# Folding the first MLP weight into Nyström attention, with coarser loads and merged attention pieces

## The chip, the core and the metric

The kernel runs on one core of one Trainium2 chip. The metric is device time in microseconds (us) for one execution. Each number for a kernel is the median of several executions; its profile is one further execution under the hardware profiler.

Engine names in the profile: PE is TensorE (matmuls), PEld its weight loads, DVE VectorE, ACT ScalarE, POOL GpSimd, SP the sync engine that issues some transfers. "L98" is line 98 of the kernel that the line comes from. The profile also records the clock granted to TensorE, 1.0 being full speed. In the code, PSUM tiles are what the matmuls write, and a tile's first dimension, 128 at most here, is its partitions.

## The reference

The operation is Nyström attention (8 batches, 8 heads, 576 tokens, 64 features per head, 32 landmarks) followed by an MLP with a squared ReLU (512 to 2048 to 512 features). Cut to what matters:

```python
q_lm = q.reshape(B, H, 32, 18, D).mean(axis=3)      # landmarks: means of 18 tokens
k_lm = k.reshape(B, H, 32, 18, D).mean(axis=3)
A  = softmax(q    @ k_lm.T / 8)      # 576 x 32
Bm = softmax(q_lm @ k_lm.T / 8)      # 32 x 32
C  = softmax(q_lm @ k.T    / 8)      # 32 x 576
Z  = Bm.T / (norm_1(Bm) * norm_inf(Bm) + 1e-6)      # 1-norm, inf-norm
for _ in range(6):                   # Newton steps towards the inverse of Bm
    Z = 2 * Z - Z @ Bm @ Z
x  = (A @ Z @ C @ v)                 # per head; then heads side by side: 4608 x 512
h  = x @ w_in                        # 4608 x 2048
return (relu(h) ** 2) @ w_out        # 4608 x 512
```

## The kernel before

Each batch of attention forms `xT` (x transposed, in bf16) for 576 tokens; the MLP then runs over nine blocks of 512 tokens. A "quad" is four heads whose 32 landmarks fill the 128 partitions. Inside a quad the Newton steps work on one 128x128 block-diagonal matrix.

The MLP block: MLP-in is 64 matmuls (4 feature tiles x 16), MLP-out is another 64. Both take their PSUM tile from the same two buffers ("mo").

```python
    def moe_superblock(t0, ntok):
        gT = moep.tile([P, D_FF // P, TOK_SB], BF16, tag="gT", bufs=1)
        for f in range(D_FF // P):
            hps = psum.tile([P, TOK_SB], F32, tag="mo", bufs=2)
            for kt in range(D_MODEL // P):
                nc.tensor.matmul(hps[:, 0:ntok], lhsT=w_in_bf[:, kt, f*P:(f+1)*P],
                                 rhs=xT[:, kt, t0:t0+ntok], start=..., stop=...)
            ... relu on ScalarE into r_sb, square on VectorE into gT[:, f, :] ...
        for ts0 in range(0, ntok, P):
            ops = psum.tile([P, D_MODEL], F32, tag="mo", bufs=2)
            ... 16 matmuls gT x w_out_bf, ScalarE copy, store ...
```

The loads: q and k come as bf16 through the software queue in pieces of 64 elements; v comes as f32 through the sync engine and is cast on VectorE.

```python
        for c in range(NCH):                       # 4 chunks of 128 tokens, one of 64
            nc.gpsimd.dma_start(qbf[:rows, c, :, :], q[b, :, s0:s0+rows, :].rearrange("h s d -> s h d"))
            ... the same for kbf ...
        vstg = qkv.tile([P, NCH, H, D], F32, tag="vstg")
        nc.vector.memzero(vstg[64:128, NCH - 1, :, :])
        for c in range(NCH):
            nc.sync.dma_start(vstg[:rows, c, :, :], v[b, ...])
        nc.vector.tensor_copy(v_aug[:, :, :, 0:D], vstg[:])
```

The attention works head by head on 32 partitions where it fills or reads the diagonal blocks:

```python
            BDB = quadp.tile([P, P], F32, tag="BDB")
            nc.vector.memzero(BDB[:])
            for h4 in range(4):
                nc.vector.tensor_scalar(out=BDB[32*h4:32*h4+32, 32*h4:32*h4+32],
                    in0=Ebm[32*h4:32*h4+32, :], scalar1=rrb[32*h4:32*h4+32, :], op0=ALU.mult, ...)
            # ... Newton steps; then, for C v:
            for g in range(4):
                nc.vector.reciprocal(rrc[32*g:32*g+32, :], cvps[32*g:32*g+32, ...])
            for g in range(4):
                nc.vector.tensor_scalar(out=cvq[32*g:32*g+32, :], in0=cvps[32*g:32*g+32, ...],
                                        scalar1=rrc[32*g:32*g+32, :], op0=ALU.mult, ...)
            nc.vector.memzero(wbd[:])
            for i in range(2):
                wps = ...                              # one matmul
                nc.scalar.copy(wbd[64*i:64*i+32, 0:D], wps[0:32, :])
                nc.scalar.copy(wbd[64*i+32:64*i+64, D:2*D], wps[32:64, :])
```

The softmax here doesn't subtract the row's maximum and nothing guards it: scores larger than these inputs give would overflow.

## Time and profile before

| | before |
|---|---|
| median of 4 runs | 468.79 us (466.21 to 471.53) |
| median in the rounds beside the changed kernel (16 runs) | 470.28 us |
| span of the profiled execution | 467.4 us |
| mean granted clock of TensorE | 0.963 |

These are lines of the profile page of the kernel before. The first gives the span, the second busy time, share of the span and instruction count of each engine; then comes TensorE's busy share in 40 slices of 11.7 us in tenths, and the sizes of the transfers' packets.

```profile
span 467.4 us, 7392 instructions
PE 395.1 (85%) x2720; PEld 196.3 (42%) x2720; DVE 259.1 (55%) x803; ACT 199.7 (43%) x541; POOL 71.5 (15%) x92
...
PE   0215678999989998999899989997989898999996
...
DMA packets 120324, 32.98 MB, mean 71 GB/s; under 512 B 113120, under 2 KB 115168, under 8 KB 120288
```

TensorE looks busy for 85% of the time, but "busy" counts each matmul's full duration in the trace: a matmul of 32 columns is recorded as 0.19 us long, where dense ones start 25 ns apart. A better measure is what dense matmuls need. The end of the run has nothing but the MLP. This is the timeline of TensorE there (start, duration, engine, line, operation, output and inputs, shape, count):

```profile
407.90 13.99 PE L98 MATMUL hps<-xT,w_in_bf 128*128 128x512 bf16 x64
421.72 13.98 PE L112 MATMUL ops<-w_out_bf,gT 128*128 128x512 bf16 x64
```

From start to start, 64 matmuls of 512 columns take 13.82 us: 216 ns each. The Trainium skill, page "TensorE: Matmul & The Clock Gate", section "Wait — 56ns, not 53.3ns?", gives N / 2.4 GHz + 2.5 ns per matmul of N columns with a floor near 25 ns. The trace agrees: 216, 56 and 25 ns for 512, 128 and 32 columns. I call the sum of these costs over all matmuls the **issue work**. It is an estimate (the few f32 matmuls are counted like bf16, and matmuls that start together are counted one by one): 324.6 us before. The rest of the span, 142.8 us, is **lost**: TensorE waits, or runs at a lower clock.

Where it is lost, by stretches: 50.6 us in the first 57 us, 32.7 us from 57 to 155 us, 11.6 us in the steady period of 48.5 us after that, 10.7 to 11.1 us in each of the next four. The two stretches of that first steady period follow, from the windows view of the kernel before. The columns are the stretch, its length, busy time and count of PE, PEld, DVE, ACT and POOL, the granted clock, the DMA share and GB/s.

```profile
155.04:169.00 13.96, 13.96 (x66) 6.23 (x65) 2.32 (x6) 2.35 (x5) 0.00 (x0) 1.00 0.60 142
169.00:203.50 34.50, 30.74 (x261) 16.10 (x261) 28.91 (x93) 20.63 (x61) 8.39 (x10) 0.95 0.56 43
```

The first stretch is MLP-out, one dense block, with 0.3 us lost. The second holds attention with MLP-in between: 23.3 us of issue work in 34.5 us, 11.2 us lost. VectorE is busy for 28.91 of those 34.5 us.

What happens in the start is shown by TensorE's longest wait there (view of waits: who waited for whom, us in total, times, longest) and by the timeline of VectorE before it:

```profile
PE bmps L183 <- DVE BD L173: 11.0, 1, 11.0
```
```profile
12.67 1.62 DVE L152 CAST v_aug<-vstg 128x2560 bf16<-128x2560 f32 x1 [5.78 <-DMA vstg<-in_v_dram]
...
33.59 1.49 DVE L152 CAST v_aug<-vstg 128x2560 bf16<-128x2560 f32 x1 [9.24 <-issue]
...
35.74 0.42 DVE L172 CAST BD<-means_ps 64x256 bf16<-64x256 f32 x1
```

The means were done by 25.07 us, but their copy (BD) started only after the second cast of v had run. That cast is for batch 1 (the cast for batch 0 ran at 12.67 us); the last of the transfers that it needs landed at 33.51 us. So attention of batch 0 cannot begin its scores before 35.7 us: it waits in VectorE's queue for a load that it does not need. Most of the 25 us before that went on waiting for q and k; the last piece of k landed at 24 us.

### The profile page before, as it was taken

Reading aid. Unit: us, or ns where it says so; the run is one execution under the profiler, and the core shown is the slowest. Engines: PE = TensorE matmul, PEld = TensorE weight load, DVE = VectorE, ACT = ScalarE, POOL = GpSimd, SP = SyncE. Lnnn points to the kernel's source line nnn. Section 1 sums busy time; section 2 is a strip of 40 time slices with the busy share of each in tenths; the row PEclk is TensorE's granted clock in tenths of the full one; section 3 lists DMA queues with packets and bytes.
Section 4 is the critical chain, followed back from the end, with each engine's and each line's share of the span. In section 5 each row is a group of like instructions: output and inputs, shape, how many; then the busy total and the mean of one; then the engine's idle time right before and its main releaser. Section 6 shows DMA issues by size and latency. Waiting matters only on the chain.

```text
span 467.4 us, 7392 instructions
## 1 busy us (share of the span) xinstructions
PE 395.1 (85%) x2720; PEld 196.3 (42%) x2720; DVE 259.1 (55%) x803; ACT 199.7 (43%) x541; POOL 71.5 (15%) x92
## 2 busy tenths in 40 slices
PE   0215678999989998999899989997989898999996
PEld 0013345344534543444354435443535443444442
DVE  4128578782678448853886288719750976041220
ACT  1012335562556254634463357325742574272541
POOL 8412070070007000600052003300000000000000
PEclk9999988799989998999899989999999989999999
DMA  9999999096109810991069204920002000101101
GB/s 157 169 194 158 185 176 132 2 95 153 46 1 86 142 67 1 61 165 69 1 45 72 78 1 29 75 82 9 1 1 87 5 1 1 67 24 45 45 25 67
DMA packets 120324, 32.98 MB, mean 71 GB/s; under 512 B 113120, under 2 KB 115168, under 8 KB 120288
## 3 DMA queue, kind: packets, MB, share of 16 engines
q0 software_dynamic: 77600, 13.64, 37.7%
q1 hardware_dynamic: 42688, 18.88, 17.7%
q8 instruction: 21, 0.34, 0.3%
q14 instruction: 15, 0.12, 0.1%
HBM read 36.70 MB, written 9.44 MB: 99 GB/s over the span
## 4 chain that ended last, share of the span: by engine, by line
PE 62%; DVE 17%; ACT 9%; DMA 4%; issue 4%; SPq 2%; DVEq 0%; ACTq 0%
PE ops L112 27%; PE hps L98 19%; DMA vstg<-in_v_dram 4%; PE tps L278 3%; PE ntp L250 2%; SPq L148 2%; PE ntp L246 2%; DVE stn L256 2%; PE o L362 2%; DVE rse L306 2%; DVE cvq L339 2%; DVE anorm L311 2%; ACT kT L286 2%; ACT Usb L249 2%; ACT r_sb L106 2%
## 5 line engine op out<-in xcount | busy, mean ns | idle before, releaser
L98 PE MATMUL hps<-xT,w_in_bf 128*128 128x512 bf16 x576 | 165.4, 398 | 1.6 <-ACT r_sb L106 1.4
L112 PE MATMUL ops<-w_out_bf,gT 128*128 128x512 bf16 x576 | 125.9, 379 | 0.1
L106 ACT ACTIVATE r_sb<-hps 128x512 bf16<-128x512 f32 x144 | 85.5, 603 | 39.6 <-PE hps L98 25.9
L107 DVE TENSOR_TENSOR gT<-r_sb 128x512 bf16<-128x512 bf16 x144 | 59.2, 422 | 46.6 <-ACT r_sb L106 45.2
L112 PEld LDWEIGHTS <-gT 128*128 128x128 bf16 x576 | 56.3, 98 | 67.8 <-DVE gT L107 0.5
L98 PEld LDWEIGHTS <-w_in_bf 128*128 128x128 bf16 x576 | 53.9, 102 | 45.8 <-issue 10.7
L135 POOL DMA_DIRECT2D qbf<-in_q_dram x40 | 35.9, 897 | 207.1 <-PE tps L278 201.7
L120 ACT COPY o_sb<-ops 128x512 f32<-128x512 f32 x36 | 21.1, 586 | 102.8 <-PE ops L112 102.8
L284 DVE COPY qT<-tps 128x640 bf16<-128x640 bf16 x32 | 15.4, 488 | 62.2 <-PE tps L278 61.1
L249 ACT CAST Usb<-ntp 128x128 bf16<-128x128 f32 x96 | 25.2, 266 | 47.3 <-PE ntp L246 45.5
L139 POOL DMA_DIRECT2D kbf<-in_k_dram x40 | 35.2, 880 | 14.5 <-DMA w_in_bf<-in_moe_w_in_dram 9.4
L256 DVE SCALAR_TENSOR_TENSOR stn<-stn,ntp 128x256 bf16<-128x256 bf16 x64 | 26.2, 421 | 11.8 <-PE ntp L253 6.3
L246 PE MATMUL ntp<-stn,BDBT_sb 128*128 128x128 bf16 x80 | 19.9, 248 | 7.6 <-DVE stn L256 6.5
L250 PE MATMUL ntp<-stn,Usb 128*128 128x128 bf16 x80 | 19.9, 257 | 7.5 <-ACT Usb L249 6.5
L250 PEld LDWEIGHTS <-Usb 128*128 128x128 bf16 x96 | 9.9, 103 | 37.2 <-ACT Usb L249 36.1
L286 ACT COPY kT<-tps 128x640 bf16<-128x640 bf16 x32 | 22.2, 697 | 7.4 <-PE tps L278 7.2
L369 DVE CAST xT<-o 128x512 bf16<-128x512 f32 x32 | 21.8, 691 | 5.4 <-PE o L362 4.3
L278 PE MATMUL tps<-ident_bf,kbf 128*128 128x128 bf16 x160 | 17.1, 234 | 6.1 <-DMA kbf<-in_k_dram 6.1
L161 PE MATMUL means_ps<-seg_bf,qbf 128*128 128x32 bf16 x160 | 9.2, 180 | 14.1 <-DMA qbf<-in_q_dram 13.9
L152 DVE CAST v_aug<-vstg 128x2560 bf16<-128x2560 f32 x8 | 12.0, 1503 | 15.1 <-issue 9.2
L339 DVE TENSOR_SCALAR cvq<-cvps,rrc 32x64 bf16<-32x64 f32 x64 | 18.0, 281 | 1.9
L172 DVE CAST BD<-means_ps 64x256 bf16<-64x256 f32 x8 | 3.3, 412 | 26.2 <-ACT STk L169 26.2
(85 smaller groups left out, 429.8 us busy)
## 6 DMA issues: line engine op xcount, KB each, us to landing
out_dram<-o_sb SPq DMA_DIRECT2D x36, 256.0 KB, 2.0
vstg<-in_v_dram SPq DMA_DIRECT2D x32, 256.0 KB, 6.3
qbf<-in_q_dram POOLq DMA_DIRECT2D x32, 128.0 KB, 4.5
kbf<-in_k_dram POOLq DMA_DIRECT2D x32, 128.0 KB, 4.6
w_in_bf<-in_moe_w_in_dram POOLq DMA_DIRECT2D x1, 2048.0 KB, 22.3
w_out_bf<-in_moe_w_out_dram POOLq DMA_DIRECT2D x1, 2048.0 KB, 24.5
vstg<-in_v_dram SPq DMA_DIRECT2D x8, 128.0 KB, 6.4
qbf<-in_q_dram POOLq DMA_DIRECT2D x8, 64.0 KB, 4.1
```

The source lines that it names most:

```text
L98: nc.tensor.matmul(hps[:, 0:ntok], lhsT=w_in_bf[:, kt, f * P:(f + 1) * P], rhs=xT[:, kt, t0:t0 + ntok], start=(kt == 0), stop=(kt == D_MOD ...
L106: nc.scalar.activation(r_sb[:, 0:ntok], hps[:, 0:ntok], AF.Relu)
L107: nc.vector.tensor_tensor(gT[:, f, 0:ntok], r_sb[:, 0:ntok], r_sb[:, 0:ntok], ALU.mult)
L112: nc.tensor.matmul(ops[0:m, :], lhsT=gT[:, f, ts0:ts0 + m], rhs=w_out_bf[:, f, :], start=(f == 0), stop=(f == D_FF // P - 1),)
L135: nc.gpsimd.dma_start(qbf[:rows, c, :, :], q[b, :, s0:s0 + rows, :].rearrange("h s d -> s h d"),)
L139: nc.gpsimd.dma_start(kbf[:rows, c, :, :], k[b, :, s0:s0 + rows, :].rearrange("h s d -> s h d"),)
L246: nc.tensor.matmul(Ups[:, :], lhsT=BDBT_sb[:, :], rhs=BDZ, start=True, stop=True)
L249: nc.scalar.copy(Usb[:], Ups[:])
L250: nc.tensor.matmul(VTps[:, :], lhsT=Usb[:, :], rhs=BDZT, start=True, stop=True)
L256: nc.vector.scalar_tensor_tensor(out=stn[:, :], in0=st[:, :], scalar=2.0, in1=ntp[:, P:3 * P], op0=ALU.mult, op1=ALU.subtract)
L278: nc.tensor.transpose(tps[:, 128 * c:128 * c + 128], tbf[:, c, 2 * p:2 * p + 2, :].rearrange("p h d -> p (h d)"), ident_bf[:],)
L286: nc.scalar.copy(tT[:], tps[:])
```

## The change

The intent: x is never needed by itself. With A the normalized scores and W = Z C v, h = A (W w_in), so w_in can be folded into attention: G = (Z C v) w_in per batch has 256 landmark rows (8 heads x 32), and the first GEMM contracts over 256 rows instead of 512 features. The same rewrite changes more:

- q, k and v are loaded with four consecutive tokens per partition ("(p c)"), in runs of 1 KB in memory, all as bf16 through the software queue; VectorE reorders q and k with one copy each; the output is stored in the same token order.
- Both quads share ops where possible. The per-head pieces on 32 partitions become one op on 128 partitions with a mask.
- MLP-out has a PSUM buffer of its own; one MLP-in tile holds 576 tokens; two batches share nine output tiles.

The diff, cut to its core (names shortened where the kernel unpacks them):

```diff
-            nc.gpsimd.dma_start(qbf[:rows, c, :, :], q[b, :, s0:s0+rows, :].rearrange("h s d -> s h d"))
-            nc.sync.dma_start(vstg[:rows, c, :, :], v[b, ...])          # f32, cast later
-        nc.vector.tensor_copy(v_aug[:, :, :, 0:D], vstg[:])
+            nc.gpsimd.dma_start(raw[:], src[b, :, 0:512, :].rearrange("h (p c) d -> p h c d", c=4))
+            nc.vector.tensor_copy(nat[:, 0:4, :, :], raw.rearrange("p h c d -> p c h d"))
+        nc.gpsimd.dma_start(vm[:], v[b, :, 0:512, :].rearrange("h (p c) d -> p h c d", c=4))
...
-            for h4 in range(4):
-                nc.vector.tensor_scalar(out=BDB[32*h4:32*h4+32, 32*h4:32*h4+32], ...)
+            nc.vector.scalar_tensor_tensor(out=st[:, 1, :, :], in0=spread(Bn, qd),
+                    scalar=rc[:, qd:qd+1], in1=blk[:], op0=ALU.mult, op1=ALU.mult)
...
-            for g in range(4): nc.vector.reciprocal(rrc[32*g:32*g+32, :], ...)
-            for g in range(4): nc.vector.tensor_scalar(out=cvq[32*g:32*g+32, :], ...)
+            nc.vector.reciprocal(rc2[:], cv[:, 4*D:4*D+1])
+            nc.vector.scalar_tensor_tensor(out=cvb[:], in0=cv[:, 0:4*D]..., scalar=rc2[:],
+                    in1=mask4..., op0=ALU.mult, op1=ALU.mult)
...
-            o512 = A-transposed x W per head pair, copied to xT
+        for n in range(4):
+            for qd in range(2):
+                for i in range(2):      # G = W w_in
+                    nc.tensor.matmul(g[64*i:64*i+64, :], lhsT=WT[:, 2*qd+i, :],
+                                     rhs=w_in_bf[:, 2*qd+i, n*512:n*512+512], start=True, stop=True)
+                ... copy g to G: ScalarE for quad 0, VectorE for quad 1 ...
...
-            for kt in range(4):
-                nc.tensor.matmul(hps, lhsT=w_in_bf[:, kt, f*P:(f+1)*P], rhs=xT[:, kt, t0:t0+512], ...)
+            for qd in range(2):
+                for j in range(2):
+                    nc.tensor.matmul(h[:, j, 0:288], lhsT=G[:, qd, f*P:(f+1)*P],
+                                     rhs=AT[:, qd, j*288:(j+1)*288], ...)
...
-            ops = psum.tile([P, D_MODEL], F32, tag="mo", bufs=2)
+            ops = psum.tile([P, DM], F32, tag="o", bufs=1)
```

## The prediction

> **What bounds the kernel now.** Matmul issue on PE, with large holes. In the last 60 us (timeline of PE) each block of 64 matmuls of 512 columns takes 13.82 us: 216 ns each. The Trainium skill, "TensorE: Matmul & The Clock Gate", section "Wait — 56ns, not 53.3ns?", gives N / 2.4 GHz + 2.5 ns, with a floor near 25 ns; the trace agrees (56 ns for 128 columns, about 30 for 64, 25 for 32). Counting all matmuls so, I estimate 40.8 us of issue per batch, 326 us in all, of 467. About 141 us are lost:
> - Start: dense MLP work begins at about 57 us (timeline), behind loads in 256 B pieces (113,120 of 120,324 packets are under 512 B), BD waiting to 35.7 us behind the v cast in VectorE's queue (chain of waits), and the Newton loop's latency. About 45 us.
> - Steady state: period 48.5 us ("ops" blocks start at 155.0, 203.5), about 39 us of PE work in it: MLP-out is one dense block, then attention runs at the pace of VectorE and ScalarE. About 9 us per batch.
> - Granted clock 0.97: about 10 us.
>
> **What the change does.** It folds w_in into attention: G = (Z C V) w_in per batch, so the first GEMM contracts over 256 landmark rows, not 512 features: 15.5 to 7.8 us per batch (64 matmuls of 288 columns). G costs 16 matmuls of 512, 3.5 us; attention's output matmuls go (1.1 us). I estimate 35.5 us per batch, 284 in all: 42 us less PE.
> ScalarE: relu takes 128 x about 660 ns (603 for 512 columns now): still 85 us. G adds 2.4 us ScalarE and 2.8 us VectorE per batch. VectorE loses the v cast (1.5), the 32-partition pieces (about 5.4) and xT (2.7); it gains two copies raw to nat (1 to 1.5 each). I estimate ScalarE 24 and VectorE 30 us per batch, VectorE not far below PE.
> Loads come in runs of 1 KB (the skill, "DMA: Bandwidth & Descriptors", Specifications: line rate from 512 B; no run here has shown it yet), all through the software queue, weights ahead of batch 1.
> Attention(b+1) now precedes MLP(b) in program order, so the MLP fills attention's waits.
>
> **On the critical path.** Start: q and k of batch 0 near 11 us, attention(0) about 23 us, so MLP(0) from about 35 us. 15.5 MB of first loads at about 300 GB/s end near 50 us; attention(1) begins only then and finishes near 80; MLP(0) is used up near 62: a second hole at 62 to 80 us. Afterwards 39 to 42 us per batch (35.5 / 0.97, and 5 to 10% lost to chain latency, the one output PSUM buffer, and MLP-in paced by relu, 0.66 against 0.49 us). Sum: 284 work, 20 start, 25 steady, 8 clock, 8 tail: about 345 us. Range 318 to 378. Faster by over 2%: 0.97; within: 0.02; slower: 0.01.
>
> **What would show it.** Right: 512 first-GEMM matmuls of 288 columns, near 122 ns apart; MLP(0) starting at 30 to 40 us; batch-1 loads landing near 50 us and a PE hole before MLP(1); period 39 to 42 us; packets mostly of 512 B and more. Wrong: period near 45 us with VectorE or ScalarE ending most PE waits; gaps of 0.9 us between output tiles.
>
> **What would make it wrong.** Too high, if loads are faster or attention hides fully. Too low, if the single queue starves attention(1) past 60 us, if VectorE becomes the pacer, or if a denser PE is throttled more.

## The result

| | before | after |
|---|---|---|
| median in the same rounds | 470.28 us (16 runs) | 350.97 us (10 runs, 349.86 to 353.14) |
| ratio, 95% interval | | 0.7473 (0.7451 to 0.7496) |
| span of the profiled execution | 467.4 us | 351.4 us |
| mean granted clock | 0.963 | 0.970 |
| issue work (estimate) | 324.6 us | 282.5 us (268.6 us with G's pairs counted once) |
| lost (span less issue work) | 142.8 us | 68.9 us (82.8 us) |

A ratio here is the mean time of one kernel's runs over that of the other's runs in the same rounds, so it is not quite the ratio of the medians quoted. The outputs are right.

The kernel is faster by a quarter, and the prediction (345 us, 318 to 378) held. But the fold removes 42 us of issue work by the count, and the time fell by 119 us. More than half of the gain must be time no longer lost.

The count is too high for the new kernel. The two matmuls of a pair in G (64 columns each, writing the two halves of g's partitions) start 3 ns apart, in all 64 pairs. This is the timeline of TensorE; the next matmul after these six starts at 189.42 us:

```profile
188.65 0.84 PE L351 MATMUL g<-w_in_bf,WT 128*64 128x512 bf16 x6
```

Six matmuls of 512 columns took 0.77 us; one after another they would take 1.30 us. So G costs 1.7 us per batch and not 3.5, and with its pairs counted once the issue work falls by 56 us, not 42. That is still less than half of 119. The losses of the new kernel given below are by the plain count; each batch adds 1.7 us to them.

The page of the new kernel, the same lines as before, with the granted clock in tenths added (a slice is 8.8 us):

```profile
span 351.4 us, 6957 instructions
PE 315.9 (90%) x2768; PEld 184.4 (52%) x2768; DVE 213.2 (61%) x546; ACT 169.3 (48%) x377; POOL 45.6 (13%) x68
...
PE   0286899899999998999999998999999998999995
...
PEclk9995589999999999999999999999999999999999
...
DMA packets 47136, 28.23 MB, mean 80 GB/s; under 512 B 13824, under 2 KB 42496, under 8 KB 47104
```

VectorE has 257 fewer instructions and 46 us less busy time, although it took over the two reordering copies and half of G. The windows of the new kernel (columns as before): the start, the next stretch, and two batches of the steady state:

```profile
0.00:42.60 42.60, 21.21 (x202) 14.51 (x203) 20.07 (x59) 11.32 (x28) 20.38 (x36) 0.81 1.26 178
42.60:80.00 37.40, 36.02 (x330) 20.11 (x329) 28.56 (x72) 22.24 (x49) 6.45 (x8) 0.94 0.90 115
156.96:235.86 78.90, 76.05 (x694) 44.63 (x693) 52.06 (x133) 41.50 (x94) 9.36 (x12) 1.00 0.49 76
```

The steady state takes 39.45 us per batch and loses about 4.2 us of it. (A period of the kernel before contains a block of 512 tokens, one of the new kernel a batch of 576, so the two periods are not the same amount of work; the loss can be compared.) In the start 32.4 us are lost up to 42.6 us, where MLP-in begins, and 6.2 us from there to 80 us.

The two large matmul groups and the relu of the new kernel (groups view: line, engine, operation, count, busy us and mean ns of one, idle before and its releaser):

```profile
L382 PE MATMUL ops<-w_out_bf,gT 128*128 128x512 bf16 x576 | 145.7, 380 | 1.1 <-DVE o_sb L388 1.1
L369 PE MATMUL h<-AT,G 128*128 128x288 bf16 x512 | 91.3, 288 | 3.1 <-ACT r L373 2.3
L373 ACT ACTIVATE r<-h 128x576 bf16<-128x576 f32 x128 | 81.3, 657 | 11.8 <-PE h L369 10.5
```

The 512 MLP-in matmuls are there. Their spacing is read at the end of the run (timeline of TensorE of the new kernel): eight of them in 0.98 us, 122.5 ns each.

```profile
322.59 1.14 PE L369 MATMUL h<-AT,G 128*128 128x288 bf16 x8
323.57 0.38 PE L382 MATMUL ops<-w_out_bf,gT 128*128 128x512 bf16 x1
```

The start has a new longest wait (view of waits). It is not for q or k, but for the constant matrix that forms the means (q was in place at 12.53 us, so the constant itself costs 0.9 us at most):

```profile
PE means L171 <- DVE seg L124: 13.4, 1, 13.4
```

### The profile page after: what moved, and what is told of

It reads as the page before. It is cut to its first block, busy times and chain, and to the rows that moved or that the text cites. A ratio compares the mean times of both kernels' runs of the same rounds, so it can differ in the third digit from the quotient of the medians.

```text
span 351.4 us, 6957 instructions
## 1 busy us (share of the span) xinstructions
PE 315.9 (90%) x2768; PEld 184.4 (52%) x2768; DVE 213.2 (61%) x546; ACT 169.3 (48%) x377; POOL 45.6 (13%) x68
## 4 chain that ended last, share of the span: by engine, by line
PE 72%; ACT 14%; issue 4%; DVE 4%; DMA 3%; POOL 1%; DVEq 0%; ACTq 0%; POOLq 0%
PE ops L382 33%; PE h L369 15%; PE g L351 6%; PE tps L233 4%; ACT r L373 4%; PE cv L325 3%; PE nt L278 3%; ACT tT L241 3%; DMA raw<-in_q_dram 3%; DVE stn L284 2%; PE means L171 2%; ACT EA L259 2%; ACT EC L259 2%; PE nt L275 2%; ACT U L277 2%
## 5 line engine op out<-in xcount | busy, mean ns | idle before, releaser
L382 PE MATMUL ops<-w_out_bf,gT 128*128 128x512 bf16 x576 | 145.7, 380 | 1.1 <-DVE o_sb L388 1.1
L369 PE MATMUL h<-AT,G 128*128 128x288 bf16 x512 | 91.3, 288 | 3.1 <-ACT r L373 2.3
L373 ACT ACTIVATE r<-h 128x576 bf16<-128x576 f32 x128 | 81.3, 657 | 11.8 <-PE h L369 10.5
L374 DVE TENSOR_TENSOR gT<-r 128x576 bf16<-128x576 bf16 x128 | 54.6, 449 | 13.3 <-ACT r L373 12.4
L369 PEld LDWEIGHTS <-G 128*128 128x128 bf16 x512 | 45.4, 98 | 20.3 <-issue 9.3
L277 ACT CAST U<-nt 128x128 bf16<-128x128 f32 x96 | 23.5, 269 | 19.2 <-PE nt L275 18.0
L358 DVE CAST G<-g 128x512 bf16<-128x512 f32 x32 | 22.1, 691 | 11.0 <-PE g L351 10.6
L241 ACT COPY tT<-tps 128x576 bf16<-128x576 bf16 x32 | 20.1, 637 | 18.0 <-PE tps L233 17.9
L284 DVE SCALAR_TENSOR_TENSOR stn<-stn,nt 128x256 bf16<-128x256 bf16 x64 | 24.6, 417 | 3.2 <-PE nt L281 1.8
L351 PE MATMUL g<-w_in_bf,WT 128*64 128x512 bf16 x128 | 21.7, 421 | 1.4 <-DVE WT L343 1.4
L278 PEld LDWEIGHTS <-U 128*128 128x128 bf16 x96 | 9.3, 97 | 23.3 <-ACT U L277 20.1
```

The source lines that it names most:

```text
L241: nc.scalar.copy(tT[:, p, :], tps[:, 0:S])
L277: nc.scalar.copy(U[:], nt[:, 0:P])
L278: nc.tensor.matmul(nt[:, 2 * P:3 * P], lhsT=U[:], rhs=st[:, P:2 * P], start=True, stop=True)
L284: nc.vector.scalar_tensor_tensor(out=stn[:], in0=st, scalar=2.0, in1=nt[:, P:3 * P], op0=ALU.mult, op1=ALU.subtract)
L351: nc.tensor.matmul(g[64 * i:64 * i + 64, :], lhsT=WT[:, 2 * qd + i, :], rhs=w_in_bf[:, 2 * qd + i, n * 512:n * 512 + 512], start=True, sto ...
L358: nc.vector.tensor_copy(dst, g[:])
```

## The experiments

Twelve kernels ran. All outputs are right. The main question: which parts of the change earn the 77 us beyond the 42 us of issue work (63 us beyond 56 with G's pairs counted once)? The theories, which are rivals for this time:

- the fold is worth its issue work and no more, or it is worth more because it relieves other engines;
- v's cast in VectorE's queue costs time in the start only, or in every period;
- VectorE's 32-partition pieces hold up attention in every period, or they lie in the shade of the matmuls;
- MLP-out as a dense block keeps MLP-in from filling attention's waits;
- the load pieces of 256 B, or the half clock in the start, set the time of the first batches.

Each ratio is to the kernel before in the same rounds. Letters in the expectations name theories.

### 1. The new kernel with only the fold undone

```diff
-        G = attn.tile([P, 2, DFF], BF16, tag="G")       # G = (Z C v) w_in, 16 matmuls of 512 columns, two side by side
+        G = attn.tile([P, NPAIR, S], BF16, tag="G")     # x transposed, 8 matmuls of 288 columns
+                nc.tensor.matmul(g[:], lhsT=WT[64*i:64*i+64, qd, :],
+                                 rhs=AT[64*i:64*i+64, qd, j*HALF:(j+1)*HALF], start=True, stop=True)
...
-            for qd in range(2):
+            for kt in range(NPAIR):
-                    nc.tensor.matmul(h[:, j, 0:HALF], lhsT=G[:, qd, f*P:(f+1)*P], rhs=AT[:, qd, ...])
+                    nc.tensor.matmul(h[:, j, 0:HALF], lhsT=w_in_bf[:, kt, f*P:(f+1)*P], rhs=G[:, kt, ...])
```

> The new kernel with the fold alone undone: the attention output x is formed (8 matmuls of 288 columns per batch in place of 16 of 512 for G) and the first GEMM contracts over 512 features again (128 matmuls of 288 columns per batch in place of 64). Issue work by my count rises from 282 to about 326 us. Theory A, PE issue time is on the critical path nearly one for one: 385 to 400 us. Rival B, the fold is small beside the filled holes and the added matmuls fall into waits: at most 365 us.

Measured: 400.64 us, ratio 0.8518 (0.8498 to 0.8538). Issue work 326.2 us, lost 72.8 us. So the fold is worth 49.7 us. By the plain count it saves 43.7 us of issue work; with matmuls that start together counted once in both kernels, some 56 us (an estimate). It is real, and most of it is on the critical path, as expected (the time is just above the upper end of the range). But 70 us of the gain have nothing to do with the fold.

### 2. The kernel before, with v loaded as bf16 straight into place

```diff
-        vstg = qkv.tile([P, NCH, H, D], F32, tag="vstg")
-        nc.vector.memzero(vstg[64:128, NCH - 1, :, :])
-            nc.sync.dma_start(vstg[:rows, c, :, :], v[b, ...])
+            nc.gpsimd.dma_start(v_aug[:rows, c, :, 0:D], v[b, ...])
-        nc.vector.tensor_copy(v_aug[:, :, :, 0:D], vstg[:])
```

> The kernel before, with v loaded as bf16 straight into v_aug by the software queue, so VectorE loses the v cast (1.5 us) and a memset (0.5 us) per batch. Theory C, VectorE paces the attention phase (it is 84% busy in the 34.5 us where PE loses 11 us, and 17% busy in the 14 us MLP-out block) and its queue holds back BD at the start: BD copies at 25 to 28 us in place of 35.7, steady period shorter by 1.5 to 2 us, time 446 to 458 us. Rival D, the latency of the Newton loop and PE's order set the period: only the start gains, 460 us or more, period 48.4 us still.

Measured: 449.70 us, ratio 0.9562 (0.9539 to 0.9585): 20.6 us faster. The period stays at 47.9 to 48.7 us. Nearly all of the gain lies in the start. The timeline of VectorE of this kernel shows the same copy as above, 20 us earlier:

```profile
15.77 0.42 DVE L172 CAST BD<-means_ps 64x256 bf16<-64x256 f32 x1 [0.34 <-ACT STk L169]
```

The expectation had this copy at 25 to 28 us. It came earlier because two things changed. The wait of TensorE for BD fell from 11.0 to 0.6 us. And the means themselves were done 9.6 us sooner, as their first copy on ScalarE shows (timeline of ScalarE, the kernel before, then this one):

```profile
25.07 0.27 ACT L169 CAST STk<-means_ps 128x128 bf16<-128x128 f32 x1 [22.97 <-PE means_ps L161]
```
```profile
15.47 0.27 ACT L169 CAST STk<-means_ps 128x128 bf16<-128x128 f32 x1 [13.38 <-PE means_ps L161]
```

With v no longer loaded as f32 through the sync engine's queue beside them, q and k of batch 0 landed sooner. So about half of the 20 us is the cast in VectorE's queue and half is the load; no run took the cast away and left the load where it was. The first MLP-in matmul moves from 58.5 to 40.1 us. The total met the range of the theory that the cast also costs time in every period, but for another reason; with the period unchanged that theory falls. The cast costs 1.5 us of VectorE per batch and none of it is on the steady chain.

### 3. The kernel before, with its 32-partition pieces merged

The four pieces of BDB, the four reciprocals and four scalings of cvq become one masked op each; the four copies of wbd become one.

```diff
-            nc.vector.memzero(BDB[:])
-            for h4 in range(4):
-                nc.vector.tensor_scalar(out=BDB[32*h4:32*h4+32, 32*h4:32*h4+32], ...)
+            nc.vector.scalar_tensor_tensor(out=BDB..., in0=Ebm... .to_broadcast([P, 4, M_LM]),
+                scalar=rrb[:], in1=blk[:], op0=ALU.mult, op1=ALU.mult)
...
-            for g in range(4): nc.vector.reciprocal(rrc[32*g:32*g+32, :], ...)
-            for g in range(4): nc.vector.tensor_scalar(out=cvq[32*g:32*g+32, :], ...)
+            nc.vector.reciprocal(rrc[:], cvps[:, D:D + 1])
+            nc.vector.scalar_tensor_tensor(out=cvq[:], in0=cv4[:, :, 0:D], scalar=rrc[:],
+                in1=mask4... .to_broadcast([P, 4, D]), op0=ALU.mult, op1=ALU.mult)
...
-                nc.scalar.copy(wbd[64*i:64*i+32, 0:D], wps[0:32, :])          # four copies per quad
-                nc.scalar.copy(wbd[64*i+32:64*i+64, D:2*D], wps[32:64, :])
+            nc.scalar.copy(wbd[:], wps[:])
```

> The kernel before with attention's 32-partition pieces merged as in the new kernel: BDB in one masked operation in place of a memset and four, the four reciprocals and four scalings of cvq in one each, W in one eviction. About 3.7 us less VectorE per batch, all of it in the serial chain before and after the Newton loop, and about 1 us less ScalarE. Theory I, the steady loss in the kernel before is attention's chain of small pieces: period 44 to 46.5 us in place of 48.4, time 440 to 456 us. Rival D, the latency of the Newton loop sets it: period still above 47.5 us, time 462 us or more (an off-chain cut of 2 us of VectorE left the period at 48.4).

Measured: 422.15 us, ratio 0.8996 (0.8968 to 0.9025), against 469.86 us before: 47.7 us faster, more than the range said. The issue work hardly changes (325.5 us by the count); the period falls from 48.5 to 42.0 us and the loss in it from 11.6 to 4.8 us.

Why so much? First what the pieces cost. These are VectorE's groups in the kernel before, then in this kernel:

```profile
L339 DVE TENSOR_SCALAR cvq<-cvps,rrc 32x64 bf16<-32x64 f32 x64 | 18.0, 281 | 1.9
L198 DVE TENSOR_SCALAR BDB<-Ebm,rrb 32x32 f32<-32x32 f32 x64 | 15.1, 235 | 1.2
...
L336 DVE RECIPROCAL rrc<-cvps 32x1 f32<-32x1 f32 x64 | 10.4, 162 | 1.6 <-PE cvps L326 0.2
```
```profile
L339 DVE SCALAR_TENSOR_TENSOR cvq<-cvps,rrc,mask 128x256 bf16<-128x256 f32 x16 | 7.6, 475 | 0.2
L203 DVE SCALAR_TENSOR_TENSOR BDB<-Ebm,rrb,blk 128x128 f32<-128x128 f32 x16 | 5.6, 352 | 0.5
...
L338 DVE RECIPROCAL rrc<-cvps 128x1 f32<-128x1 f32 x16 | 2.6, 160 | 0.7 <-PE cvps L328 0.6
```

A reciprocal of 32 partitions takes 162 ns, one of 128 partitions 160 ns. Writing 16 times the elements of one piece of cvq at once (most of them zeros from the mask) takes 475 ns instead of 4 x 281. In these figures the number of partitions made no difference; what an op cost went with its length along a partition, and with a fixed part. The Trainium skill, "VectorE: DVE Perf Modes", section "The TRN2 errata — SBUF-src ops pay a fixed extra latency per instruction", says that "many small tiles pay it per-tile"; these numbers agree. (The page says it of sources in SBUF, as BDB's; cvq reads PSUM and behaves alike.)

Together the pieces cost 43.5 us of VectorE before and 15.8 us merged: 27.7 us in all, 3.5 us per batch. That alone cannot be 47.7 us of time. The rest is in what TensorE does meanwhile. This is the chain of waits of the kernel before in one steady period (start, us, what; pieces are left out, among them two whole-tile ops of VectorE of 0.7 us each):

```profile
171.43 0.23 DVE BDB L198
...
171.67 0.23 DVE BDB L198
...
171.92 0.23 DVE BDB L198
...
172.16 0.24 DVE BDB L198
...
176.06 0.17 DVE rrc L336
...
178.00 0.27 ACT Usb L249
...
178.32 0.23 PE ntp L250
...
178.70 0.43 DVE stn L256
...
179.18 0.23 PE ntp L246
...
179.43 0.27 ACT Usb L249
```

From 171.2 to 177.7 us every step of the chain is on VectorE. While that lasts TensorE still has MLP-in to do: 13 of its matmuls run from 171 to 177.2 us, and only 1.9 us are lost. The damage comes after. From 177.7 us on, the Newton steps (ntp, Usb, stn) follow one another with nothing between them: each step waits for ScalarE, TensorE and VectorE in turn. In the kernel with merged pieces the Newton steps look like this (the same view):

```profile
163.67 0.06 PE ntp L248
163.73 0.65 PE hps L105 x3
164.38 0.16 PE ntp L252
...
164.65 0.43 PE hps L105 x2
165.08 0.16 PE ntp L252
```

MLP-in (hps) stands between the Newton matmuls, and the chain runs on TensorE. The order of TensorE's matmuls is the compiler's, so I compared the compiled orders, and counted how many Newton matmuls stand in a row with no other matmul between (the 33 of the first batch left aside, which has no MLP to mix in; the order of the matmuls in the traces gives the same counts):

```
kernel                              longest rows of Newton matmuls in the compiled order
before                              three rows of 21, four of 19
before, v straight                  seven rows of 21
before, control of experiment 5     one of 19, six of 15
before, pieces merged               one of 10, then none over 3
before, both edits                  none over 3
new, fold undone                    none over 4
new                                 one of 6, then none over 4
```

So the edit did two things: it shortened the chain, and it let the compiled order mix MLP-in into the Newton steps. The windows show what a row of 19 costs. First the kernel before, in the row and just after it; then ten microseconds of Newton steps in the kernel with merged pieces:

```profile
177.20:182.00 4.80, 2.84 (x20) 1.24 (x20) 4.46 (x13) 2.19 (x7) 0.00 (x0) 1.00 0.00 0
182.00:185.40 3.40, 3.40 (x15) 1.66 (x14) 2.42 (x8) 1.83 (x5) 0.00 (x0) 0.50 0.02 5
```
```profile
160.00:170.00 10.00, 9.77 (x65) 3.91 (x64) 7.98 (x22) 7.35 (x22) 0.00 (x0) 1.00 0.01 2
```

In the 4.8 us of the row the kernel before has 1.28 us of issue work: 3.5 us lost, and 3.2 to 3.3 us in the next two periods. Then comes the second half of the bill: after the thin stretch the clock is granted at half for 3.4 us, just when MLP-in fills TensorE again; 1.5 us are lost. The merged kernel loses 1.8 us in ten microseconds, at full clock. The row and the half clock together are 5.0 of the 11.6 us lost per period before; the loss fell by 6.8 us.

The half clock comes back in every period: the record of the kernel before has six stretches of 3.41 us, 47.8 us apart, and two of 6.83 us before them. The kernel of experiment 2, which keeps the pieces, has the six as well. The kernel with merged pieces has one of 3.41 us and 1.4 us in its last moments. The Trainium skill, "TensorE: Matmul & The Clock Gate", sections "What's actually happening" and "HAM oscillation — how this bites in real kernels", describes a window of 3.41 us and a half clock after idleness; the trace agrees in the length and the factor. As an estimate, half of the half-clock time is lost: 17 us before and 2 us here, so up to 15 of the 47.7 us came back as clock. A long row does not always bring it on: in the test of experiment 5, rows of 16 and 14 matmuls are followed by half clock in one case each, and not in the other.

Two things stay open. No run held the compiled order fixed while it merged the pieces, so the shares of the shorter chain and of the new order were not taken apart; and the four copies of wbd on ScalarE went with the rest.

### 4. Both small edits in the kernel before

The edits of experiments 2 and 3 in one kernel, to see whether they add up and what is left for the rest of the rewrite.

> The kernel before with both small edits: attention's pieces merged, and v loaded straight into v_aug. The gains alone were 47.7 us (mostly a steady period of 42.0 in place of 48.4 us) and 20.6 us (all in the start). If they are separate causes they add up: 397 to 407 us, the same as the new kernel without the fold (400.6 us), so that the fold's 50 us is what is left. If they are two views of one cause: 415 us or more.

Measured: 401.12 us, ratio 0.8519 (0.8479 to 0.8559). Alone the edits gave 20.6 and 47.7 us, together 70.4 us: they add up. And 401.12 us is the time of the new kernel with its fold undone (400.64 us). So the whole gain is accounted for:

| step | us | gain |
|---|---|---|
| before (in its rounds) | 470 to 471.5 | |
| v straight as bf16: the start | | 20.6 |
| merged 32-partition pieces: the steady state | | 47.7 |
| both | 401.1 | 70.4 |
| new kernel with the fold undone | 400.6 | |
| the fold | | 49.7 |
| the new kernel | 351.0 | |

The rest of the rewrite (loads in 1 KB runs, the token order, one more PSUM buffer, the tiles of 576) is needed for the fold or comes out near zero in sum; parts of it can offset each other (experiment 5 finds 9.6 us for the PSUM buffer). Experiments 5 to 8 look at the parts that could have mattered.

### 5. PSUM buffers and dense blocks

In the kernel before MLP-out comes as one dense block of 64 matmuls, for MLP-in and MLP-out take turns on two buffers. In the new one MLP-out has its own buffer and is spread in blocks of 16 or fewer between attention's ops. To see what this is worth, MLP-out got a buffer of its own in the kernel before, at the price of one of attention's buffers; a control pays the price alone.

```diff
# control: attention's buffers 3 -> 2, everywhere
-                    tps = psum.tile([P, SP], BF16, tag="ts", bufs=3)
+                    tps = psum.tile([P, SP], BF16, tag="ts", bufs=2)
# the test: as the control, and
-            ops = psum.tile([P, D_MODEL], F32, tag="mo", bufs=2)
+            ops = psum.tile([P, D_MODEL], F32, tag="oo", bufs=1)
# the opposite, in the new kernel
-            ops = psum.tile([P, DM], F32, tag="o", bufs=1)
+            ops = psum.tile([P, DM], F32, tag="h", bufs=2)
```

The control:

> A control: the kernel before with two instead of three PSUM buffers for attention's wide tiles (one bank left unused), which frees the bank that the next run uses. The compiled order already breaks a few of the nine 64-matmul MLP-out blocks (longest runs 56, 57, 64). Expected 463 to 480 us on every theory.

Measured: 464.60 us, ratio 0.9879 (0.9831 to 0.9927). One buffer fewer does no harm; it even gains a little.

The test:

> The same, with MLP-out in that freed bank as its only buffer, apart from MLP-in's two. In the compiled order MLP-out now falls into blocks of 16 and less, with attention and MLP-in between them. Theory H, the steady loss of 11 us per batch comes from attention being shut out of PE while 64 MLP-out matmuls run, and from MLP-out not being at hand as a filler in the Newton loop: 425 to 450 us, period of 42 to 46 us per batch. Rival I, the loss is attention's own chain of small VectorE pieces, wherever it stands: within 2% of the control.

Measured: 457.57 us, ratio 0.9739 (0.9704 to 0.9774). The compiled order does change (23 blocks of 16 and small ones instead of nine blocks of 64), yet it gains only 7.0 us over the control, 1.5%. The theory that the dense blocks cause the steady loss mostly falls. The rows of Newton matmuls are a little shorter here (two of 16, two of 14, the rest shorter), and they still cost. The half-clock stretches shrink from 35.9 to 20.4 us between the two profiled executions, which would explain up to 7.7 us (an estimate, half of the difference). So the spread blocks may help mainly by keeping the clock up; no run tested this.

The opposite:

> The new kernel with MLP-out in MLP-in's two PSUM buffers instead of in its own single one. In the compiled order MLP-out then runs in blocks of 44 to 60 matmuls. Theory H: the two-batch period grows from 78.9 to 86 to 95 us, time 372 to 400 us. Rival I (the new kernel's chain is short enough to be hidden anyway): at most 358 us.

Measured: 360.56 us, ratio 0.7677 (0.7643 to 0.7711): 9.6 us slower than the new kernel, two batches take 82.3 us instead of 78.9. It fell between the two theories. In both kernels the own buffer is worth some 1.5 to 1.7 us per batch; it is a detail of the new kernel's gain, not its cause.

### 6. VectorE's queue in the new kernel

The new kernel reorders q and k with two copies on VectorE per batch, 1.4 us. The first kernel here makes each copy three times; the second moves them to GpSimd.

```diff
-            nc.vector.tensor_copy(nat[:, 0:NC4, :, :], raw.rearrange("p h c d -> p c h d"))
+            for _ in range(3): nc.vector.tensor_copy(nat[:, 0:NC4, :, :], raw.rearrange(...))
# the other kernel
+            nc.gpsimd.tensor_copy(nat[:, 0:NC4, :, :], raw.rearrange("p h c d -> p c h d"))
```

> The new kernel with the copies from raw to nat made three times over for batches 1 to 7 (2.8 us more VectorE per batch, same result). Theory C, VectorE paces the attention and MLP-in phase: the two-batch period grows from 78.9 to 83 to 84.5 us, time 363 to 371 us. Rival E, VectorE at 61% busy has slack: at most 355 us.

Measured: 366.37 us, ratio 0.7791: 15.4 us slower for 16.9 us more of VectorE's busy time. Two batches take 82.0 us: in the steady state 2.4 us of added work per batch cost 1.6 us. Some 6 of the 15.4 us have arisen by 141 us, where this trace has 10.24 us of half clock (from 66.9 us) that the new kernel lacks.

> The new kernel with the copies from raw to nat of batches 1 to 7 on GpSimd in place of VectorE (1.4 us less VectorE per batch). If VectorE paces attention as the run with added copies showed (15 us more for 19 us more of copies), then 342 to 348 us; if the copies cost VectorE's queue nothing where they stand, or GpSimd is too slow or holds back the loads behind it, 350 us or more.

Measured: 354.50 us, ratio 0.7543 (0.7521 to 0.7564): the steady state does not move (two batches again 78.9 us) and the start loses about 3 us. GpSimd needs 1.89 us for what VectorE does in 0.69 (timeline of GpSimd of this kernel), which may be why:

```profile
97.36 1.89 POOL L160 COPY knat<-raw 128x2048 bf16<-128x2048 bf16 x1
```

So more work in VectorE's queue costs about two thirds of its length in the steady state, while moving work off it gained nothing. VectorE is busy for 66% of the steady state, so its throughput alone does not set the pace. The second kernel is no clean test of less work, since the copy got slower; why nothing was gained was not tested further.

### 7. The size of the load pieces

The loads of q, k and v in the new kernel, cut into four transfers of 256 B pieces each.

```diff
-            nc.gpsimd.dma_start(raw[:], src[b, :, 0:NC4*P, :].rearrange("h (p c) d -> p h c d", c=NC4))
+            pieces = src[b, :, 0:NC4*P, :].rearrange("h (p c) d -> p h c d", c=NC4)
+            for c in range(NC4):
+                nc.gpsimd.dma_start(raw[:, :, c, :], pieces[:, :, c, :])
```

> The new kernel with q, k and v loaded in pieces of 256 B again, four transfers in place of one. Theory F, runs of 1 KB shorten the start: q of batch 0 lands 2 to 4 us later than 11.8 us, batch 1 later than before, time 354 to 360 us. Rival G, the first loads are limited by bytes, not by pieces, and the rest is hidden: within 1% of the new kernel, 348 to 354 us.

Measured: 359.46 us, ratio 0.764 (0.7616 to 0.7664): 8.5 us slower, all of it in the start. But the pieces are not what costs: q of batch 0 was copied at 12.65 us instead of 11.84. The timeline of GpSimd of this kernel shows why the means began at 20.1 us instead of 13.45:

```profile
5.60 3.55 POOL L82 DMA_DIRECT2D raw<-in_q_dram  x4
...
19.55 0.24 POOL L114 TENSOR_SCALAR_AFFINE_SELECT seg_f<-seg_f 128x32 f32<-128x32 f32 x1
```

Each issue of a transfer holds GpSimd for about 0.9 us here, and GpSimd also builds the constant seg, behind all of the issues. To take this apart, a second kernel builds the constants before it issues the weights' transfers.

```diff
+    # constants (identity, seg, masks) built here
     for j in range(4):
         nc.gpsimd.dma_start(w_in_bf[:, :, j*512:(j+1)*512], ...)
-    # constants built here
```

> The kernel with loads in 256 B pieces, with the constants built before the weights' loads are issued. In the earlier run with 256 B pieces q of batch 0 had landed by 12.6 us (11.8 with 1 KB), but means began at 20.1, behind seg, which POOL built only after issuing 12 more loads at 0.9 us each. Theory J, POOL's issue time and not the piece size cost the 8 us: means begin near 15.5 us, 353 to 356 us. Theory F, the piece size: still 358 us or more.

Measured: 358.45 us, ratio 0.763 (0.7593 to 0.7667). The means begin at 16.9 us, 3.2 us earlier, and MLP-in at 46.2 instead of 49.4 us, but the time gains only 1.0 us and the intervals of the two overlap. The range expected was not met. By the times this is settled only in part: q came 0.8 us later with the smaller pieces, and the issues cost far more. The traces say more about the rest. In both kernels the means still waited for seg (ready at 20.07 and 16.88 us) while q was in place at 13.35 and 13.12 us, for the second kernel builds its constants behind the issues of q, k and v all the same. Between the profiled executions the first kernel is 7.0 us longer than the new one, with means 6.7 us later; the second is 5.0 us longer, with means 3.5 us later. So most of the cost is the late constant; the last 1.5 us stay open. (The medians lie further apart, 8.5 and 7.5 us, for the profiled execution of the new kernel was its slowest.)

### 8. Clock in the start of the new kernel

The record of the new kernel has one long stretch of half clock, 20.48 us, from 26.5 to 47 us. To keep the clock up, 24 matmuls of 512 columns with no use were put between the Newton steps of batch 0.

```diff
+                if b == 0:
+                    for _ in range(2):
+                        nc.tensor.matmul(warm[:], lhsT=U[:], rhs=w_in_bf[:, 0, 0:512], start=True, stop=True)
```

> The new kernel with 24 matmuls of 512 columns, whose result nobody reads, between the steps of the first Newton loop. Theory K, the granted clock of 0.5 between 26.5 and 47 us of the new kernel costs time: with PE kept busy the clock stays at 1.0, MLP-in of batch 0 begins at 39 to 41 us in place of 42.6, time 345 to 349 us. Rival L: the first 47 us are bound by the chain's latency on the other engines and the half clock costs nothing: 350 us or more.

Measured: 351.38 us, ratio 0.7493 (0.7468 to 0.7518). The half clock now ends at 31.75 us and the mean of the record is 0.99. It gains nothing: MLP-in of batch 0 begins at 44.5 instead of 42.6 us, so the extra matmuls probably delay the chain of batch 0, and MLP-in of batch 1 begins at 77.5 us, against 77.3. That fits a start bound by the chain of attention's small steps and not by clock. But the delay from the extra matmuls and any gain from the clock were not taken apart.

None of these kernels beats the new one.

## Why the prediction was right

The total was right: 351 us for 345 predicted, well inside 318 to 378. That it came so close is partly luck. 284 us of work and 61 us of losses were predicted; with G's pairs counted once it was 268.6 us of work and 82.8 us of losses, and the two errors cancel. Step by step:

- **Issue work: right but for G.** 284 us predicted; the same formula gives 282.5 for the compiled matmuls, which checks the count and not the chip. MLP-in is 512 matmuls of 288 columns, 122.5 ns apart, as said. G was put at 3.5 us per batch and took 1.7, since its matmuls run in pairs. Undoing the fold alone cost 49.7 us, where 42 us less work was predicted, so the saving itself is shown on the chip.
- **Steady period: right in size, wrong in its cause.** 39 to 42 us were predicted and 39.45 measured. The prediction said "Attention(b+1) now precedes MLP(b) in program order, so the MLP fills attention's waits". The second half is what the trace shows: MLP-in now stands between the Newton steps. The first half is a misreading: the kernel before emits its MLP blocks with a lag (`MOE_LAG` in its source), so that attention of batch 1 already precedes the first block there. What let the MLP fill the waits were the merged pieces: experiment 3 has it without any change to the loop. The prediction had these pieces as 5.4 us of VectorE's busy time per batch to be subtracted, not as what kept MLP-in out of the Newton steps.
- **Start: right in direction, too low.** 20 us lost were predicted; 32.4 us were lost before MLP-in began, and 6.2 us up to 80 us. MLP-in of batch 0 began at 42.6 us, not at 30 to 40: the means waited until 13.45 us for the constant seg, and attention of batch 0 took 29 us instead of 23. On the other side the second hole at 62 to 80 us did not appear, for MLP-in of batch 0 began later and was stretched by attention of batch 1, until about 80 us.
- **Loads: slower predicted than measured.** The first loads were expected near 50 us, at 300 GB/s; q, k and v of batch 1 had landed by 44.95 us. In the stretch below, from the windows of the new kernel, 199 GB/s are written as bf16; the reads are f32, so twice that, about 400 GB/s, is read.

```profile
30.00:40.00 10.00, 7.55 (x52) 4.44 (x51) 5.35 (x15) 1.60 (x6) 2.90 (x4) 0.50 1.41 199
```

- **The BD copy behind the v cast: right.** The prediction named it as one reason for the late start; of the 20.6 us of experiment 2, some 10.4 are this wait and 9.6 are q and k landing sooner. The prediction laid the loads to pieces of 256 B, but there the pieces stayed and only v's loads changed.
- **VectorE and ScalarE: too high.** 30 and 24 us per batch predicted, 26.7 and 21.2 measured. The reordering copies took 0.69 us, not 1 to 1.5; the relu took 657 ns, as said.
- **Clock: right by the mean, not by its effect.** The record's mean is 0.97, but it is one stretch in the start; of it only 42.6 to 47 us holds dense work. In the steady state the clock is now full, where the prediction carried the old average over. It missed that in the kernel before half clock followed each long row of bare Newton steps from 80 us on.
- **Packets: right in size, small in worth.** Packets below 512 B fell from 113,120 to 13,824. By experiment 7 that is not where the time went.
- **Gaps of 0.9 us between output tiles,** named as a sign of being wrong, did not show: all of the waits of MLP-out for its single buffer sum to 1.1 us in its group.

## What to carry to other kernels

Look in the chain of waits for runs of small ops on one engine: four ops on 32 partitions took two to four times as long as one op on 128, and merging them can also change the compiled order, so look there for long rows of dependent matmuls with no filler, and at the clock just after them. Look also for what stands ahead of the first useful op in an engine's queue: a cast for the next batch, waiting for its load, held up the first batch by some 10 us here, and the load itself held back q and k by about as much. Look at start times before adding up matmuls: pairs that start together cost half. And check an accounting by building the old kernel up and the new one down: here they met at 401 us, which left 50 us for the clever part and 70 us for two small edits.

## What the Trainium skill lacked or had wrong

- "TensorE: Matmul & The Clock Gate", section "What's actually happening", gives half clock as the default state. The runs agree, but the recorded clock does not show it: the new kernel's record begins at 23.1 us and counts as full before, while 20 transposes of 128 columns from 17.69 to 19.82 us stand 106.5 ns apart, twice the 56 ns of later ones. The page's caveats on the record do not say that its start can be missing and that a mean clock is then too high.
- The same page ties the return to half clock to idleness over a window, and elsewhere to frequent short idles. Here TensorE had matmuls in flight for 2.84 of the 4.8 us before (1.28 us of issue work), and still went to half clock for 3.41 us, once per period of 47.8 us. How thin is too thin is not stated.
- The same page says of the warm-up that "the ramp penalty is <1% of a typical kernel span". In the kernel before, half-clock stretches came to 34.9 of 467 us, up to 17 us or 3.7% lost; they were not the ramp at the start, but returns. The sentence holds for one ramp; the returns, which the page treats apart, are no matter of 1%.
- "VectorE: DVE Perf Modes" has the fixed cost per instruction, but no example on few partitions: 32x1 and 128x1 reciprocals took 162 and 160 ns, four 32x64 scalings 4 x 281 ns, one masked 128x256 op 475 ns.
- "DMA: Bandwidth & Descriptors", section "Anatomy of one DMA — SWDGE (gpsimd) path", in its table of where the time goes, calls the generation of descriptors "small, variable". Each issue held GpSimd for 0.7 to 1.0 us in these runs, and delayed the constants that GpSimd builds by 6.7 us in experiment 7.
- The same page, "Specifications", gives about 358 GB/s from HBM per core, as half of what two cores share. This program ran on one core, and about 400 GB/s were read over 10 us (an estimate: 199 GB/s written as bf16 from f32), so the row is no limit for such a core. Its 512 B for line rate did not decide here: with 256 B pieces the first q was copied 0.8 us later.
- "GPSIMD Engine Reference", section "Engine selection", says that ops with one input run roughly at line rate. The bf16 copy of 128x2048 took 1.89 us on GpSimd and 0.69 us on VectorE.
